# The first two token groups of a fused attention and expert kernel take turns in halves, with an order table found beforehand

## Chip, cores and metric

The kernel runs on one core of a Trainium2 chip. The metric is the device time of one execution in microseconds (us); the median of several runs is quoted. Engines are named as the profile names them: PE is TensorE (matmuls), PEld its weight loads, DVE is VectorE, ACT is ScalarE, POOL is GpSimd, SP is SyncE, which issues nearly all DMAs.

## What is computed

Attention with a compressive memory on 4 batches, 8 heads, 576 tokens and head size 64, followed by a gated expert layer on the 2304 tokens:

```
a       = softmax(causal(q k^T / 8));   local = a v
q_p     = phi(q)                        # phi(x) = elu(x) + 1
mem_out = (q_p M_prev) / (q_p z_prev)
x       = sigmoid(beta) * mem_out + (1 - sigmoid(beta)) * local     # [2304, 512]
out     = (sigmoid(x Wg) * (x Wv)) Wo                               # d_ff = 1536, out [2304, 512]
```

The expert weights arrive as 64-bit floats and are converted on the chip.

## The kernel before

**Work.** The 2304 tokens are cut into 6 groups of 384. Groups 1 to 4 are the first 384 tokens of each batch; groups 0 and 5 are "tail" groups that join the last 192 tokens of two batches. Attention of a group goes by 4 pairs of heads, 24 pairs (numbers 0 to 23) in all. For each pair `scores` (L577 matmuls in plain f32) writes scores to PSUM banks, DVE masks and takes the row extreme (L641), ACT takes the exponential (L653), the result is turned, `values` multiplies by v (L336), `scaled` normalises into `xs` with the small row factors `rs`, `recall` does the same for the memory term `xm` (row factors `rn`). `across` turns the finished 384x128 block into `xh` and `xl`, a high and a low half in the fast 32-bit matmul format, for the expert layer. For pairs 0 to 7 both turns go through PE (L339, against the identity `idn`), for pairs 8 to 23 through DMA transposes (`planes`).

**Experts.** A group then takes 12 expert steps of 128 hidden units each (`moe`). A step is 33 matmuls: 12 for the gate and 12 for the value (128x384, high and low halves of `x` and of the weights), and 9 for the output product ("down", 128x512), which accumulate over all 12 steps in three PSUM banks (0 to 2), one for each 128 tokens. Between them ACT takes a tanh and DVE and ACT make `th`, `gh`, `gl` (L941, L943, L345, L355). The down matmuls of a step stand after the gate and value matmuls of the next one. At a group's end the three sums go through ACT to `ob`, a ring of two buffers, and out by DMA. Group 0 and the last group go through the three sums in the order 2, 0, 1, the others 0, 1, 2.

**Weights.** In group 0 each step's three weight blocks are loaded and converted (`convert`: one ACT pass, L850, L852 and L855 on DVE, then a split into halves by a cast on ACT and a subtraction on DVE). The gate weights `wg` stay in SBUF; value and output weights live in a ring `sv` of three buffers, and their converted f32 form is written to DRAM (`w`). Later groups load it back (`sv<-w`, 512 KB) and split it again. Groups go through the steps upwards and downwards by turns, so that the three last steps' buffers are still there for the next group.

**Order.** The code records every operation in `Program` with an engine, a cost, the data it depends on and a place in the order. A list scheduler then goes through it: whenever an engine is free, the ready operation with the lowest place goes next, and the engines' instruction queues are emitted in that order. In the kernel before, a search at build time (`plan`, `replay`, `issue`) moves places to and fro against three modelled worlds (`SEARCH`, `WORLDS`) and keeps the best. The recording loop at the end of the program interleaves attention of group g+1 with the expert steps of group g, paced so that it is done when the 12 steps are.

Of the kernel before, what the change touches and what calls it, by code (L numbers as in the profile page):

```python
# [25 lines left out]
AHEAD = 8  # L26


# [6 lines left out]
ROUNDS = 1  # L35

SEARCH = (260.0, 1500), (1e9, 300)

WORLDS = (380.0, 1.2, 0.0, 0.0), (385.0, 1.2, 0.03, 0.6), (370.0, 1.2, 0.03, 1.2)
# [14 lines left out]
class Program:  # L54
# [63 lines left out]
    def plan(self, order, until):  # L118

        ops, cost, kbs, engine, users = self.ops, self.cost, self.kbs, self.engine, self.users  # L120
        rate, lag, _, _ = self.worlds[0]
        push, pop = heapq.heappush, heapq.heappop
        left = list(self.left)
        ready_at = [0.0] * len(ops)
        free = [START] * 5
        link = 0.0
        coming, ready = [[] for _ in range(5)], [[] for _ in range(5)]
        for i, n in enumerate(left):
            if not n:
                push(coming[engine[i]], (0.0, i))  # L130
        made = []
        while True:
            at, e = 1e9, -1
            for x in range(5):
                t = free[x]
                if not ready[x]:
                    c = coming[x]
                    if not c:
                        continue
                    if c[0][0] > t:  # L140
                        t = c[0][0]
                if t < at:
                    at, e = t, x
            if e < 0 or free[PE] > until:
                return made
            c, r = coming[e], ready[e]
            while c and c[0][0] <= at:
                k = pop(c)[1]
                push(r, (order[k], k))
            i = pop(r)[1]  # L150
            done = at + (cost[i] * 1.5 if e == PE and at < COLD else cost[i])
            free[e] = done
            if kbs[i]:
                link = done = max(link, done + lag) + kbs[i] / rate
            made.append(i)
            for u, wake in users[i]:
                t = done + wake
                if t > ready_at[u]:
                    ready_at[u] = t
                left[u] -= 1  # L160
                if not left[u]:
                    push(coming[engine[u]], (ready_at[u], u))

    def replay(self, made, world):

        rate, lag, costs, lates = world
        kbs, engine, users, pe = self.kbs, self.engine, self.users, self.cost
        n = len(self.ops)
        ready_at, start, last = [0.0] * n, [0.0] * n, [-1] * n
        free = [START] * 5  # L170
        link = 0.0
        cold = COLD
        rest = self.work
        gaps = []
        for i in made:
            e = engine[i]
            at = ready_at[i]
            c = costs[i]
            if e == PE:
                rest -= c  # L180
                if at < free[PE]:
                    at = free[PE]
                else:
                    gap = at - free[PE]
                    if gap > 0.1:
                        gaps.append((gap, i))
                        if gap > 1.3:
                            cold = max(cold, at + 2.0)
                if at < cold:
                    c *= 1.5  # L190
            elif at < free[e]:
                at = free[e]
            start[i] = at
            free[e] = done = at + c
            if kbs[i]:
                link = max(link, done + lag) + kbs[i] / rate
                done = link + lates[i]
            for u, wake in users[i]:
                t = done + wake
                if t > ready_at[u]:  # L200
                    ready_at[u], last[u] = t, i
        return max(max(free), free[PE] + rest), gaps, start, ready_at, last

    def issue(self):
        ops = self.ops
        names = sorted(WAKE)
        self.cost, self.kbs = [o[1] for o in ops], [o[2] for o in ops]
        self.engine, self.left = [names.index(o[0]) for o in ops], [len(o[4]) for o in ops]
        self.users = [[] for _ in ops]
        for i, o in enumerate(ops):  # L210
            for d in o[4]:
                self.users[d].append((i, WAKE[ops[d][0]][o[0]]))
        self.work = sum(o[1] for o in ops if o[0] == "pe")
        pick = random.Random(1)
        self.worlds = [(rate, lag, [o[1] * (1.0 + pick.random() * slip if o[0] in ("act", "dve", "pool") else 1.0) for o in ops],
                        [pick.random() ** 2 * late for _ in ops]) for rate, lag, slip, late in WORLDS]

        def trial(order, until, bar):
            made = self.plan(order, until)
            runs = []  # L220
            for w in self.worlds:
                runs.append(self.replay(made, w))
                if sum(r[0] for r in runs) > sum(bar[:len(runs)]) + (len(runs) < len(self.worlds)):
                    return None
            return [r[0] for r in runs], made, runs

        order = [o[5] for o in ops]
        for until, rounds in SEARCH:
            best = trial(order, until, [1e9] * len(self.worlds))
            for _ in range(int(rounds * ROUNDS)):  # L230
                _, gaps, start, ready_at, last = pick.choice(best[2])
                if not gaps:
                    continue
                _, i = pick.choices(gaps, [x for x, _ in gaps])[0]
                late = []
                end = start[i] - 25.0
                while i >= 0 and start[i] > end:
                    if start[i] - ready_at[i] > 0.05:
                        late.append(i)
                    i = last[i]  # L240
                if not late:
                    continue
                tried = list(order)
                for k in pick.sample(late, pick.randint(1, min(3, len(late)))):
                    by = pick.choice((20, 60, 150, 400))
                    for m in self.mates[k]:
                        tried[m] -= by
                now = trial(tried, until, best[0])
                if now:
                    best, order = now, tried  # L250
        for i in best[1]:
            ops[i][3]()
        self._best = best
        return sum(best[0]) / len(best[0])
# [3 lines left out]
def tile_attention_memory_moe(  # L258
# [522 lines left out]
    def attn():  # L781
# [10 lines left out]
        for n, x in [(n, x) for n in range(NP) for x in range(len(pairs[n].items))] + [(NP, 0)]:  # L792
# [17 lines left out]
            while len(late) > (SKEW if n < HP else n < NP):  # L810
# [3 lines left out]
                if x == len(pairs[k].items) - 1:  # L814
# [12 lines left out]
                    for y in ks:  # L827
                        across(y)
# [35 lines left out]
    def weights(F):  # L864

        g, at = divmod(F, NF)
        if g >= NG:
            return
# [199 lines left out]
```

## Time and profile before

| | us |
|---|---|
| median of 3 runs | 617.55 |
| lowest and highest run | 617.44, 620.86 |
| the profiled execution | 618.01 |
| its span, first to last instruction | 616.2 |
| PE busy in it | 603.3 (98%) |
| DVE busy | 457.9 (74%) |
| ACT busy | 316.6 (51%) |

The profiled execution ran 0.46 us longer than the median, and 1.8 us of it lie around the span. Busy time of PE counts a matmul from its start to its modelled end, and matmuls overlap: a 128x384 matmul shows 0.34 us, while the next one starts 0.17 us later. So the pace of PE is read from the starts.

### The profile page before, as it was taken

How to read it: one execution, taken by the hardware profiler on the slowest of the kernel's cores; microseconds unless marked ns; L12 is line 12 of the kernel's file. 1: busy time of each engine (PE TensorE's matmuls, PEld its weight loads, DVE VectorE, ACT ScalarE, POOL GpSimd, SP SyncE). 2: the span in 40 equal slices, each digit the busy share in tenths (PEclk: the TensorE clock that was granted, in tenths of full speed). 3: DMA queues.
4: the chain of work that ended last, by engine and by line, in shares of the span. 5: the costliest groups of instructions: out<-in, count | busy, mean ns of one | idle time of the engine just before them, and what ended most of it. 6: DMA issues, size and time to landing. Idle time of an engine off the chain costs nothing.

```text
span 616.2 us, 13289 instructions
## 1 busy us (share of the span) xinstructions
PE 603.3 (98%) x5184; PEld 528.7 (86%) x5184; DVE 457.9 (74%) x1181; ACT 316.6 (51%) x626; POOL 9.0 (1%) x51
## 2 busy tenths in 40 slices
PE   6899999999999999999999999999999999999997
PEld 3668889888888988898988899978898889999996
DVE  4899999999988777577789568689889965223432
ACT  6897867757545255245366236274555333322322
POOL 2000000000000000000000000000000000000000
PEclk9999999999999999999999999999999999999999
DMA  8578778897869454455474575668596652112231
GB/s 323 195 235 295 212 226 234 254 249 224 176 130 243 104 152 122 120 150 145 106 162 111 126 168 137 138 155 161 127 206 105 154 133 69 54 48 101 69 102 53
DMA packets 110623, 96.60 MB, mean 157 GB/s; under 512 B 79840, under 2 KB 81888, under 8 KB 110560
## 3 DMA queue, kind: packets, MB, share of 16 engines
q1 hardware_dynamic: 110416, 95.48, 59.8%
q8 instruction: 41, 0.67, 0.4%
q10 hardware_dynamic: 144, 0.26, 0.1%
q14 instruction: 22, 0.18, 0.1%
HBM read 65.84 MB, written 11.01 MB: 125 GB/s over the span
## 4 chain that ended last, share of the span: by engine, by line
PE 90%; DVE 5%; ACT 2%; issue 0%; DMA 0%; DVEq 0%
PE bank L332 75%; PE bank L336 7%; PE bank L577 5%; PE bank L339 2%; DVE a L641 1%; PE bank L534 1%; ACT a L653 1%; DVE sv L355 1%; DMA w<-wt 0%; DVE wt L852 0%; DVE xm L355 0%; DVE wt L855 0%; DVE xs L355 0%; ACT at L345 0%; DVE kq_wt L355 0%
## 5 line engine op out<-in xcount | busy, mean ns | idle before, releaser
L332 PE MATMUL bank<-xh,sv 128*128 128x384 f32 x576 | 163.3, 339 | 0.0
L332 PE MATMUL bank<-xh,wg 128*128 128x384 f32 x576 | 162.7, 340 | 0.1
L332 PE MATMUL bank<-sv,gh 128*128 128x512 f32 x432 | 138.2, 399 | 0.0
L332 PEld LDWEIGHTS bank<-xh,wg 128*128 128x128 f32 x576 | 105.3, 188 | 5.2 <-issue 0.5
L332 PEld LDWEIGHTS bank<-xh,sv 128*128 128x128 f32 x576 | 105.3, 188 | 2.1 <-issue 0.5
L943 DVE SCALAR_TENSOR_TENSOR th<-th,bank 128x384 f32<-128x384 f32 x72 | 39.8, 553 | 84.3 <-PE bank L332 84.1
L653 ACT ACTIVATE a<-a,st 128x256 f32<-128x256 f32 (+4 forms) x144 | 78.2, 580 | 39.2 <-DVE st L641 38.5
L332 PE MATMUL bank<-xl,wg 128*128 128x384 f32 x288 | 97.3, 338 | 0.0
L332 PE MATMUL bank<-xl,sv 128*128 128x384 f32 x288 | 97.0, 337 | 0.0
L666 DVE COPY at<-a 128x1024 uint16<-128x1024 uint16 (+1 forms) x144 | 86.1, 628 | 7.8 <-DMA a<-at 5.7
L332 PEld LDWEIGHTS bank<-sv,gh 128*128 128x128 f32 x432 | 79.0, 188 | 15.1 <-issue 1.0
L345 ACT CAST gh<-th 128x384 fp32r<-128x384 f32 x72 | 36.8, 512 | 97.2 <-DVE th L943 97.0
L332 PE MATMUL bank<-sv,gl 128*128 128x512 f32 x216 | 86.5, 401 | 0.0
L641 DVE CUSTOM_DVE_ANT_0 a<-bank,mask 128x512 f32<-128x512 f32 (+3 forms) x144 | 65.9, 489 | 13.1 <-PE bank L577 10.3
L941 ACT ACTIVATE th<-bank 128x384 f32<-128x384 f32 x72 | 35.2, 489 | 77.8 <-PE bank L332 75.8
L345 ACT CAST sv<-sv 128x512 fp32r<-128x512 f32 x90 | 51.2, 616 | 16.8 <-DMA sv<-w 16.5
L577 PE MATMUL bank<-kp 64*64 64x256 f32 (+4 forms) x416 | 53.8, 443 | 5.1 <-DMA kp<-in_qk_dram 4.1
L355 DVE TENSOR_TENSOR sv<-sv 128x512 fp32r<-128x512 f32 x90 | 58.1, 687 | 0.6 <-ACT sv L345 0.3
L332 PEld LDWEIGHTS bank<-xl,wg 128*128 128x128 f32 x288 | 54.1, 188 | 2.8
L355 DVE TENSOR_TENSOR gl<-th,gh 128x384 fp32r<-128x384 f32 x72 | 40.1, 557 | 19.9 <-ACT gh L345 19.1
L332 PEld LDWEIGHTS bank<-xl,sv 128*128 128x128 f32 x288 | 54.1, 188 | 0.3
L332 PEld LDWEIGHTS bank<-sv,gl 128*128 128x128 f32 x216 | 40.5, 188 | 9.3 <-DVE gl L355 0.2
(66 smaller groups left out, 600.8 us busy)
## 6 DMA issues: line engine op xcount, KB each, us to landing
sv<-w SPq DMA_DIRECT2D x45, 512.0 KB, 3.9
wr<-in_w_dram SPq DMA_DIRECT2D x36, 512.0 KB, 4.8
kp<-in_qk_dram SPq DMA_DIRECT2D x32, 384.0 KB, 3.8
w<-wt SPq DMA_DIRECT2D x24, 256.0 KB, 5.1
out_dram<-ob SPq DMA_DIRECT2D x14, 256.0 KB, 2.3
vt<-in_vp_dram SPq DMA_DIRECT2D x8, 330.0 KB, 3.7
vr<-in_vp_dram SPq DMA_DIRECT2D x8, 330.0 KB, 4.4
mb<-in_mz_dram SPq DMA_DIRECT2D x8, 260.0 KB, 5.0
```

Of the source, the lines that this page charges most:

```text
L332: lambda: nc.tensor.matmul(out=out, lhsT=lhsT, rhs=rhs, start=start, stop=stop), r, w)
L336: lambda: nc.tensor.matmul(out=out, lhsT=lhsT, rhs=rhs, start=start, stop=stop), r, w)
L339: pe(0.110, lambda: nc.tensor.transpose(out=out, in_=in_, identity=identity), r, w)
L345: act(n, lambda: nc.scalar.copy(out=out, in_=in_), r, w)
L355: dve(n, lambda: nc.vector.tensor_tensor(out=out, in0=in0, in1=in1, op=op), r, w)
L534: nc.tensor.matmul(out=sp[j][0][m0:m1, at + MC * c:at + MC * c + MC], lhsT=u.ph[r, q:q + m1 - m0], rhs=mem[u.g][e][0][r, u.p, MC * j:MC * ...
L577: nc.tensor.matmul(out=sp[j][0][m0:m1, at:at + k1 - k0], lhsT=kp[r, u.qa + q:u.qa + q + m1 - m0], rhs=kp[r, u.ka + k0:u.ka + k1], start=Tr ...
L641: dve(m + 10, lambda aj=aj, sj=sj, pj=pj, o=o, m=m, mk=mk, b=b0 + k0: nc.vector.tensor_tensor_reduce(out=aj[:, b:b + m], in0=pj[:, o:o + m ...
L653: act(W + 120, lambda aj=aj, sj=sj, b=b0, W=W: nc.scalar.activation(out=aj[:, b:b + W], in_=aj[:, b:b + W], func=AF.Exp, scale=-1.0, bias= ...
L666: dve(2 * W, lambda: nc.vector.tensor_copy(out=o, in_=i), r, w, fast=True)
L941: act(GT, lambda: nc.scalar.activation(out=th, in_=pg_[:, :GT], func=AF.Tanh, scale=0.5), [pg_k], [th_k])
L943: dve(GT, lambda: nc.vector.scalar_tensor_tensor(out=th, in0=th, scalar=1.0, in1=pv[:, :GT], op0=ALU.add, op1=ALU.mult,), [th_k, pv_k], [t ...
```

## The change

Groups 0 and 1 no longer do 12 steps each in one go. The expert work becomes a list of stages: group 0 steps 0 to 5; group 1 steps 5 to 0; group 0 steps 6 to 11; group 1 steps 11 to 6; then groups 2 to 5 with 12 steps each. A stage that only opens a group writes its three half-way sums to a DRAM buffer (`halves`); the stage that closes it loads them into `ob` and adds them to its own sums on DVE. Conversion of a weight block happens at its first use, so it is spread over four stages. `sv` buffers are now given out by least recent use. Attention of group 1 has to be complete after 6 steps of group 0; `across` of group 2 (`held`) waits until group 0 has closed, since there are two `xh` and `xl` buffers. Two modelled PE costs change, the search is gone, and a table of numbers (`MOVED`) shifts the places of single operations.

```diff
-SEARCH = (260.0, 1500), (1e9, 300)
-WORLDS = (380.0, 1.2, 0.0, 0.0), (385.0, 1.2, 0.03, 0.6), (370.0, 1.2, 0.03, 1.2)
+CUT = 6
+LINK = 380.0, 1.2
+MOVED = {
+        -6400: (1275,),
+        -800: (1202, 1276, 1700, 4596),
...
-                    pe(4 * at / 2385.0 + (0.8 if more else 0.3), together,
+                    pe(4 * at / 2385.0 + (0.36 if more else 0.32), together,
...
+        def over():
+            while held and freed:
+                across(held.pop(0))
+                yield
...
+                yield from over()
+                while held and n == 2 * HP + HP - 1:
+                    yield "wait"
+                    yield from over()
                 scores(n, x)
...
-                    for y in ks:
-                        across(y)
+                    if pairs[k].g == 2:
+                        held.extend(ks)
+                        yield from over()
+                    else:
+                        for y in ks:
+                            across(y)
...
+    low, high = list(range(CUT)), list(range(CUT, NF))
+    stages = [(0, low, True, False), (1, low[::-1], True, False), (0, high, False, True), (1, high[::-1], False, True)]
+    stages += [(g, (high + low, low[::-1] + high[::-1])[g % 2], True, True) for g in range(2, NG)]
...
+        if f in kept:
+            at = kept.index(f)
+            turns_w.remove(at)
+            turns_w.append(at)
+            ready_w[F] = next(ready_w[x] for x in range(F - 1, -1, -1) if steps_[x][1] == f)
             return
...
-        if g == 0:
+        if f not in seen:
+            seen.add(f)
...
+    halves = [dram.tile([128, GT // 128, DM], F32, name=f"part{g}") for g in range(2)]
+
+    def moe(n):
+        g, fs, opens, closes = stages[n]
...
+            if not opens:
+                load(o, halves[g][:, t], 256, [("part", g, t)], [ob_k])
+                dve(DM, lambda o=o, acc=acc: nc.vector.scalar_tensor_tensor(
+                    out=o, in0=acc, scalar=0.5, in1=o, op0=ALU.mult, op1=ALU.add), [acc_k, ob_k], [ob_k])
+                for r, q, m in rows(g, t):
+                    load(out[r:r + m, :], o[q:q + m], 2.1 * m, [ob_k], [])
+                continue
...
+            if not closes:
+                load(halves[g][:, t], o, 256, [ob_k], [("part", g, t)])
+                continue
```

The number of PE instructions is the same in both programs, kind by kind. Of the others, six casts on ACT and six subtractions on DVE for `sv`, and three loads `sv<-w`, are gone; six additions on DVE, six stores to and six loads from the half-way buffers are new.

Three places show how instructions move. The first is the start of PE's queue, after the first eight score matmuls of pair 0 (`kp0`, `kp1`). `a0` to `a5` are the exponentials, `bank` the PSUM banks, and `kp2` belongs to pair 1. Before:

```order
L339 MATMUL bank0_63<-idn_71,a0_112 128x128 x4
L339 MATMUL bank1_64<-idn_71,a1_113 128x128 x4
L577 MATMUL bank2_65<-kp2_103 128x512
L577 MATMUL bank3_66<-kp2_103 128x512
L339 MATMUL bank4_67<-idn_71,a2_116 128x128 x3
L577 MATMUL bank6_69<-kp0_101 64x256
L577 MATMUL bank7_70<-kp0_101 64x256
L577 MATMUL bank6_69<-kp1_102 64x256
L577 MATMUL bank7_70<-kp1_102 64x256
```

And now:

```order
L285 MATMUL bank0_63<-idn_71,a0_114 128x128 x4
L285 MATMUL bank1_64<-idn_71,a1_115 128x128 x3
L523 MATMUL bank6_69<-kp0_103 64x256
L523 MATMUL bank7_70<-kp0_103 64x256
L523 MATMUL bank6_69<-kp1_104 64x256
L523 MATMUL bank7_70<-kp1_104 64x256
```

The last scores of pair 0 (64x256, banks 6 and 7) now stand ahead of the first scores of pair 1. On SP the load of `bt` (beta, for the gates `gs` and `ga`) has moved as well, from the ninth place to the sixth.

The second place is DVE's queue where the last two pairs of group 1 (pairs 6 and 7) are normalised, from the first row factor `rs` on. Before:

```order
L516 SCALAR_TENSOR_TENSOR rs1_145<-bank6_69,ga_76 128x6
L516 SCALAR_TENSOR_TENSOR rs0_131<-bank5_68,ga_76 128x6
L666 COPY at0_127<-a4_120 128x512
L850 TENSOR_SCALAR wt3_148<-wt3_148 128x512
L355 TENSOR_TENSOR sv2_152<-wt2_143,sv2_152 128x512
L852 SCALAR_TENSOR_TENSOR wt3_148<-wr0_138,wt3_148 128x512
L520 RECIPROCAL rs0_131<-rs0_131 128x6
L520 RECIPROCAL rs1_145<-rs1_145 128x6
L855 SCALAR_TENSOR_TENSOR wt3_148<-wr0_138,wt3_148 128x512
L850 TENSOR_SCALAR wt0_139<-wt0_139 128x512
L355 TENSOR_TENSOR xs0_130<-bank5_68,rs0_131 128x384
L852 SCALAR_TENSOR_TENSOR wt0_139<-wr1_140,wt0_139 128x512
```

And now:

```order
L462 SCALAR_TENSOR_TENSOR rs0_133<-bank5_68,ga_76 128x6
L814 SCALAR_TENSOR_TENSOR wt3_150<-wr1_142,wt3_150 128x512
L466 RECIPROCAL rs0_133<-rs0_133 128x6
L301 TENSOR_TENSOR sv2_154<-wt1_143,sv2_154 128x512
L301 TENSOR_TENSOR xs0_132<-bank5_68,rs0_133 128x384
L462 SCALAR_TENSOR_TENSOR rs1_147<-bank6_69,ga_76 128x6
L612 COPY at0_129<-a4_122 128x512
L301 TENSOR_TENSOR xs0_132<-xs0_132,xm0_126 128x384
L466 RECIPROCAL rs1_147<-rs1_147 128x6
L612 COPY at0_129<-a5_123 128x512
L301 TENSOR_TENSOR xs1_146<-bank6_69,rs1_147 128x384
L922 SCALAR_TENSOR_TENSOR th0_151<-th0_151,bank4_67 128x384
```

Fewer pieces of weight conversion (`wt`, `sv`) stand between the parts of the normalisation. From the first `rs` to the second `xl` of these pairs the queue holds 27 instructions before, and 21 now, the one-column reads not counted.

The third place is SP's queue where group 0 is closed. Before:

```order
L671 DMA_TRANSPOSE a4_120<-at3_136 128x8x128
L363 DMA out_0_dram<-ob0_157 64x512 x2
L363 DMA out_0_dram<-ob1_158 128x512
L671 DMA_TRANSPOSE a5_121<-at3_136 128x8x128
L363 DMA out_0_dram<-ob0_157 128x512
L363 DMA vt0_108<-in_vp_dram 128x396
L363 DMA sv2_152<-w8_85 128x2x512
```

And now:

```order
L309 DMA out_0_dram<-ob0_159 64x512 x2
L309 DMA out_0_dram<-ob1_160 128x512
L309 DMA ob0_159<-part0_101 128x512
L309 DMA ob1_160<-part1_102 128x512
L309 DMA out_0_dram<-ob0_159 128x512
L309 DMA kp3_106<-in_qk_dram 128x768
L309 DMA sv0_139<-w8_85 128x2x512
```

The third half-way sum of group 0 (`part0`) is loaded into the first `ob` buffer once that one's store has landed; its own store then stands ahead of the load of k and q for a later pair and of the next weights.

## Rows read from the trace of the kernel before

**Rows 1.** The page: span, and PE's busy time, share of the span, instructions.

```profile
span 616.2 us, 13289 instructions
PE 603.3 (98%) x5184; PEld 528.7 (86%) x5184; DVE 457.9 (74%) x1181; ACT 316.6 (51%) x626; POOL 9.0 (1%) x51
```

**Rows 2.** One stretch of 20 us: busy us of PE, PEld, DVE, ACT, POOL; granted clock, DMA share, GB/s.

```profile
80.00:100.00 20.00, 20.00 (x222) 17.66 (x222) 20.00 (x55) 14.07 (x29) 0.22 (x2) 1.00 0.80 237
```

**Rows 3.** Waits of PE over the span: us in total, times, longest.

```profile
PE bank L577 <- DMA kp<-in_qk_dram: 4.1, 1, 4.1
PE bank L339 <- ACT a L653: 1.6, 3, 1.1
PE bank L332 <- DVE xm L355: 0.9, 1, 0.9
PE bank L339 <- DVE xs L355: 0.6, 1, 0.6
PE bank L577 <- DVE xm L355: 0.6, 1, 0.6
PE bank L577 <- DVE st L641: 0.3, 1, 0.3
PE bank L577 <- DVE xl L355: 0.2, 1, 0.2
```

**Rows 4.** Timeline of PE, the last matmul: start, us, instruction.

```profile
611.30 0.40 PE L332 MATMUL bank<-sv,gl 128*128 128x512 f32 x1
```

**Rows 5.** Timeline of PE, one step of the last group: its first matmul, the next step's.

```profile
546.64 0.33 PE L332 MATMUL bank<-xh,wg 128*128 128x384 f32 x1
...
552.95 0.33 PE L332 MATMUL bank<-xh,wg 128*128 128x384 f32 x1
```

**Rows 6.** Timeline from 14 to 18 us; in brackets the wait before.

```profile
14.80 0.44 PE L339 MATMUL bank<-idn,a 128*128 128x128 f32 x2 [1.14 <-ACT a L653]
...
15.47 1.09 PE L339 MATMUL bank<-idn,a 128*128 128x128 f32 x8 [0.23 <-ACT a L653]
15.79 0.21 ACT L395 ACTIVATE gs<-bt 128x8 f32<-128x8 f32 x1
...
17.14 1.39 PE L577 MATMUL bank<-kp 64*128 64x512 f32 x4 [0.57 <-DVE xm L355]
```

**Rows 7.** Groups of instructions: count, then busy us and mean ns.

```profile
L345 ACT CAST sv<-sv 128x512 fp32r<-128x512 f32 x90 | 51.2, 616 | 16.8 <-DMA sv<-w 16.5
...
L355 DVE TENSOR_TENSOR sv<-sv 128x512 fp32r<-128x512 f32 x90 | 58.1, 687 | 0.6 <-ACT sv L345 0.3
```

**Rows 8.** Timeline of the hand-over of pairs 6 and 7 to the experts.

```profile
124.56 1.57 PE L336 MATMUL bank<-vr,at 128*64 128x66 f32 x48
126.73 0.23 DVE L516 SCALAR_TENSOR_TENSOR rs<-bank,ga 128x6 f32<-128x6 f32 x2
...
137.96 0.55 DVE L355 TENSOR_TENSOR xl<-bank,xh 128x384 fp32r<-128x384 f32 x1
```

**Rows 9.** Timeline where group 0 closes: the sums leave, the next group's begin.

```profile
162.22 1.14 ACT L960 ACTIVATE ob<-bank 128x512 f32<-128x512 f32 x2
...
162.56 0.62 PE L332 MATMUL bank<-sv,gh 128*128 128x512 f32 x2
164.10 1.83 SPq L363 DMA_DIRECT2D out_dram<-ob  x3
...
167.63 0.59 ACT L960 ACTIVATE ob<-bank 128x512 f32<-128x512 f32 x1
...
169.68 0.62 PE L332 MATMUL bank<-sv,gh 128*128 128x512 f32 x2
```

**Rows 10.** DMA issues: count, KB each, median us from issue to landing.

```profile
sv<-w SPq DMA_DIRECT2D x45, 512.0 KB, 3.9
...
w<-wt SPq DMA_DIRECT2D x24, 256.0 KB, 5.1
```

**Rows 11.** The stretch around the one late wait of PE, columns as in rows 2.

```profile
405.00:420.00 15.00, 14.12 (x102) 11.61 (x102) 14.80 (x41) 9.80 (x20) 0.00 (x0) 1.00 0.56 159
```

More of the change, by code (lines that the diff above doesn't have):

```diff
@@ L116, in block @@
         self.turn = None
[L118 to L202, printed above, removed]
@@ L206, in issue @@
         names = sorted(WAKE)
-        self.cost, self.kbs = [o[1] for o in ops], [o[2] for o in ops]
-        self.engine, self.left = [names.index(o[0]) for o in ops], [len(o[4]) for o in ops]
-        self.users = [[] for _ in ops]
+        rate, lag = LINK
+        push, pop = heapq.heappush, heapq.heappop
+        order = [o[5] for o in ops]
+        for by, firsts in MOVED.items():
+            for i in firsts:
+                for m in self.mates[i]:
+                    order[m] += by
+        left = [len(o[4]) for o in ops]
@@ L210, in issue @@
+        users = [[] for _ in ops]
         for i, o in enumerate(ops):
             for d in o[4]:
[L212 to L254, printed above, removed]
+                users[d].append(i)
+        ready_at = [0.0] * len(ops)
+        free = [START] * len(names)
+        link = 0.0
+        coming, ready = [[] for _ in names], [[] for _ in names]
+        for i, n in enumerate(left):
+            if not n:
+                push(coming[names.index(ops[i][0])], (0.0, i))
+        while any(coming) or any(ready):
+            at, e = min((free[x] if ready[x] else max(free[x], coming[x][0][0]), x)
+                        for x in range(len(names)) if ready[x] or coming[x])
+            while coming[e] and coming[e][0][0] <= at:
+                k = pop(coming[e])[1]
+                push(ready[e], (order[k], k))
+            i = pop(ready[e])[1]
+            _, cost, kb, emit, _, _ = ops[i]
+            done = at + (cost * 1.5 if e == PE and at < COLD else cost)
+            free[e] = done
+            if kb:
+                link = done = max(link, done + lag) + kb / rate
+            emit()
+            for u in users[i]:
+                x = names.index(ops[u][0])
+                ready_at[u] = max(ready_at[u], done + WAKE[names[e]][names[x]])
+                left[u] -= 1
+                if not left[u]:
+                    push(coming[x], (ready_at[u], u))
@@ L779, in across @@
         keys.append([kh, kl])
+    freed = []
     def attn():
@@ L916, in down @@
                     matmul(acc, l[:, ts], r, DM, [l_k, r_k], [acc_k],
[L917 removed]
+                           f == fs[0] and i == 0, f == fs[-1] and i == 2)
                 yield
[L920 to L922 removed]
+        for at, f in enumerate(fs):
+            cur = ready_w[firsts[n] + at]
+            pz = [bank("second" if n == 0 and at == 1 else "gv") for _ in range(2)]
             turns = [(part, kd) for part in range(2) for kd in range(KD)]
[L924 removed]
+            if opens and at == 0 or n == 0 and at == 1:
                 turns = [x for x in turns if x[1] < KD - 1] + [x for x in turns if x[1] == KD - 1]
[L927 removed]
+            for m, (part, kd) in enumerate(turns):
                 pp, pp_k = pz[part]
@@ L993, in tile_attention_memory_moe @@
     lengths = [sum(2 * len(u.items) + 4 for u in pairs if u.g == g) for g in range(1, NG)] + [0]
-    def pace(g, part):
-        return sum(lengths[:g]) + part * lengths[g]
-    for g in range(NG):
+    for n, (g, fs, _, closes) in enumerate(stages):
         while ready < g:
@@ L1003, in tile_attention_memory_moe @@
                 ready = y[1]
-        for i, _ in enumerate(moe(g)):
-            while made < pace(g, (i + 1) / (7 * NF + 1)) + AHEAD and ready + 1 < NG:
+        if n < 4:
+            done_, todo = (0, lengths[0]) if n == 0 else (lengths[0], lengths[1])
+            f0, f1 = (0, CUT) if n == 0 else (firsts[n] - CUT, NF + NF - CUT)
+        else:
+            done_, todo = sum(lengths[:g]), lengths[g]
+            f0, f1 = 0, NF
+        if n == 3:
+            freed.append(True)
+        for i, _ in enumerate(moe(n)):
+            share = (f0 + (i + 1) / 7) / f1
+            while made < done_ + share * todo + AHEAD and ready + 1 < NG:
                 made += 1
                 y = step()
+                if y == "wait":
+                    break
                 if y:
```

32 lines of the change are left out of this document (14 added, 18 removed), and 39 rows, old and new, of the table MOVED.

## Prediction

> **What bounds the kernel now.** I read the page's busy line first. PE is busy for 603.3 of the 616.2 us of the span [rows 1], so the kernel can't get much faster unless PE gets less to do. The stretches of 20 us come next. From 60 to 600 us nearly all of them look like the one shown: PE 20.00 of 20 [rows 2]. DVE is just as full there, 20.00 of 20, but that costs nothing while PE has other work at hand. The third view is the list of PE's waits. The reader is to add it up: 4.1 us until the first keys and queries land, and after that 1.6 + 0.6 + 0.6 + 0.3 + 0.2 = 3.3 us in the first 50 us and 0.9 us at 415 us [rows 3]. The last matmul ends at 611.70 [rows 4], 4.5 us before the span does. So 4.1 + 3.3 + 0.9 + 4.5 = 12.8 us, which is the whole of 616.2 - 603.3. The start and the tail are in both programs. What any order can win is 4.2 us, 0.7%.
>
> Is busy time also time well spent? In the last group, with no attention left, a step takes 552.95 - 546.64 = 6.31 us [rows 5]. 72 steps at that pace are 454 us, and the order shows the same matmuls before and after. I take PE's work as unchanged.
>
> **The change part by part.** *Weights.* Three loads `sv<-w` less, and with each two casts and two subtractions: ACT loses 6 x 0.616 = 3.7 us, DVE 6 x 0.687 = 4.1 us [rows 7], and DVE gets six additions of 512 columns, 6 x 0.69 = 4.1 us, back. Conversion is spread over 24 steps in place of 12. Through the stretch in which DVE is full, PE doesn't wait at all [rows 2, 3], so a relief of DVE there is worth 0 by itself. It is cover for what the change moves forward (below).
>
> *The start.* Three of the early waits come from one knot [rows 6]. PE waits 1.14 and 0.23 us for exponentials of pair 0 whose last scores were issued behind the first scores of pair 1. Then it waits 0.57 us for banks 6 and 7, because `xm` reads them late: its gate `gs` starts on ACT only at 15.79. In the new order those scores stand ahead of pair 1's, and `bt` is loaded earlier. Both causes are gone: 1.94 us. What is late next is the first transpose of pair 1, with much the same chain behind it; I keep the other early waits (3.3 - 1.94 = 1.4) and the late 0.9, 2.3 together, as they are, less 0.5, because DVE and ACT now have less conversion ahead of the first expert step. Bounds: none of it gone (0) or all (2.3).
>
> *Group 1 is due six steps earlier.* That is 6 x 6.31 = 38 us. The last two pairs' values end on PE at 126.13, and their second `xl` on DVE ends at 138.51 [rows 8]: 12.4 us, hidden, since group 1's experts began much later. Now the order leaves between the same two points 27 gate and value matmuls, 4 down matmuls, 6 transposes and 4 score matmuls. A step's 6.31 us are about 0.175 us for each of its 24 gate and value matmuls and 0.23 for each of its 9 down matmuls; 8 transposes take 1.09 us [rows 6]. That makes 4.7 + 0.9 + 0.8, and with about 1 us for the scores 7.5 us. DVE's part shrinks from 27 instructions to 21: in proportion to the 138.51 - 126.73 = 11.8 us that the 27 took, 21 take 9.2 us, and fewer of them are conversion pieces at 0.69, so I estimate 8. The first `rs` may start 1.5 us before the values end, since it needs only the first pair's bank (half of two blocks of about 1.57). 8 - 1.5 + 0.5 of hand-over is 7.0, against 7.5. I take 0.3 us of wait. Bounds: 0, and 12.4 - 7.5 = 4.9 if DVE arrives with the backlog of before. What is queued behind on DVE are `th` and `gl` of the steps, for which PE waits next, so a late DVE isn't caught up by reordering: the order is fixed.
>
> *Half-way sums.* At a closing the third sum needs a buffer whose store has landed, then a load, then DVE. Before, at the same place, the third sum is out of its bank at 168.22, and PE wants a bank of that kind again at 169.68 [rows 9]. The last sums' matmuls begin at 162.56; about 0.7 later they end, so the store's way took 168.22 - 163.2 = 5.0 us. The load adds between 3.9 us (512 KB) and 5.1 us (256 KB) [rows 10], the addition 0.1 more than the evacuation. So the bank is free 9.0 to 10.2 us after the last down matmul, plus 0.3 of hand-over. The new order puts 41 gate and value matmuls, three down matmuls and a block of scores between, 7.2 + 0.7 + about 0.9 = 8.8 us. The wait is 0.5 to 1.7 us. It shrinks by up to 1.3 us if SP isn't busy with transposes when the first sum is ready; before, that held the store from 162.8 to 164.10 [rows 9]. In the new queue no transpose stands just ahead. I take 0.5, bounds 0 and 1.7. At group 1's closing the order leaves over 12 us, and I take 0. The two openings only store: 0, hidden as the evacuation of rows 9 is.
>
> Here a rule speaks. The Trainium skill ("DMA: Bandwidth & Descriptors", "Anatomy of one DMA — SWDGE (gpsimd) path") gives a DMA about 2.0 us and its bytes at 436 GB/s; it states it for GpSimd's path, these go through SP. By it a 256 KB load is 2.6 us, an estimate from that page, and the wait would be 0; the trace's 5.1 us for as many bytes, with other traffic in flight, differs.
>
> *Sum*, against the profiled execution: 618.01 - 1.94 - 0.5 + 0.3 + 0.5 = 616.4, and from the median, 0.46 us lower, 617.55 - 1.64 = 615.9 us. A difference under 1% (6.2 us) is about what a measurement of this kernel can't tell from no change.
>
> **The rivals.** *All waits go.* 617.55 - 4.2 = 613.3. For it: DVE and ACT are less loaded early, and the table moves hundreds of places, so it was made for this order. Against: the early attention is a chain of scores, extreme, exponential, turn, with only two pairs in flight, and it waits on each link in turn.
>
> *Nothing is gained.* The chain of the early attention is as long as before, and the 1.94 us come back at its next link: 617.55 + 0.3 + 0.5 = 618.4; with the borders hidden, 617.5. For it: the later waits of rows 3 name other links of that chain (DVE `xs`, DVE `st`).
>
> *DVE is late at the border of the first two stages: slower.* If it comes to `rs` with the backlog of before, PE stands 4.9 us there, and 1.7 at the closing: 617.55 - 1.94 + 4.9 + 1.7 = 622.2. It decides from about 1.9 us of lateness on, where the gain of the start is used up. For it: DVE was at 20.00 of 20 [rows 2] and the border is now inside that stretch. Against: six of the twelve conversions are no longer due by then.
>
> On the clock, the trace shows the granted clock at 1.00 (the 2.4 GHz level) also in the stretch with the wait of 0.9 us [rows 11], so waits of about a microsecond cost only themselves. By the Trainium skill ("TensorE: Matmul & The Clock Gate", "HAM oscillation — how this bites in real kernels") a long enough gap sends PE back to half its clock. No wait here after the start is longer than 1.14 us, so no run shows it. By that rule the slower case would cost some us more, as PE would go on at 1.2 GHz after the gap.
>
> **How the numbers follow.** Forecast, 614.4 to 617.0: 0.45. Nothing gained, 617.0 to 619: 0.20. All waits gone, under 614.4: 0.17. Slower, 619 and up: 0.18. Faster by over 1% means under 611.4, which would need more than all of PE's avoidable waits: 0.04, from the third case and PE's work being read wrongly. Slower by over 1% is above 623.7, the slower case with a second such wait: 0.08. Within 1%: 0.88. The range 612.6 to 621.0 leaves out the far ends of the third and the fourth case, together some 0.17.
>
> **What would show it.** Right: PE's busy time within 2 us of 603.3, its waits between 10 and 20 us down by about 2 us, the step of the last group still 6.31 us, waits of at most 1 us at the first border and at group 0's closing, granted clock 1.00. The steps are wrong one by one if the early waits still sum to 3.3; if PE waits for `xs`, `xl` or `th` for 2 us or more near 115 us; if it waits for `ob` near 180 us. The whole is wrong if PE's busy time changes by more than 4 us, since the argument rests on equal work.

## Result, and the profile after

The changed kernel takes 610.32 us (median of 5 runs, 610.13 to 611.24), the one before 617.93 us beside it (617.44 to 620.86): ratio 0.988, 95% interval 0.986 to 0.990. That is 1.2% faster, where faster by over 1% had a chance of 0.04, and 2.3 us under the lower end of the predicted range. The profiled execution took 611.24 us, the longest of the five, so the two profiles lie 6.8 us apart and the medians 7.6.

The page's first lines of after, which answer to [rows 1]:

```profile
span 609.5 us, 13288 instructions
PE 598.1 (98%) x5184; PEld 528.4 (87%) x5184; DVE 459.0 (75%) x1181; ACT 309.9 (51%) x620; POOL 8.4 (1%) x51
```

The span is 6.8 us shorter (616.23 and 609.45 before rounding), and 5.2 us of that are PE's *busy* time, 603.3 before [rows 1], with the same 5184 matmuls and weight loads that take as long as before (528.4 against 528.7). So PE counts as busy for longer in before, on the same work. The waits of PE in after, as in [rows 3]:

```profile
PE bank L523 <- DMA kp<-in_qk_dram: 4.1, 1, 4.1
PE bank L285 <- DVE xs L301: 0.9, 1, 0.9
PE bank L523 <- ACT at L291: 0.9, 1, 0.9
PE bank L285 <- DVE st L587: 0.9, 1, 0.9
```

Behind the first load 2.7 us are left of 4.2. This view explains 1.5 of the 6.8 us.

What the view leaves out is seen in the starts. Two stops of the kernel before, in its timeline of PE (start, us, instruction; a row with x2 holds two matmuls):

```profile
148.91 0.63 PE L332 MATMUL bank<-sv,gh 128*128 128x512 f32 x2
149.37 0.40 PE L332 MATMUL bank<-sv,gl 128*128 128x512 f32 x1
149.73 0.98 PE L332 MATMUL bank<-sv,gh 128*128 128x512 f32 x3
...
539.72 0.33 PE L332 MATMUL bank<-xl,sv 128*128 128x384 f32 x1
539.90 0.34 PE L332 MATMUL bank<-xh,sv 128*128 128x384 f32 x1
540.29 0.44 PE L332 MATMUL bank<-xh,wg 128*128 128x384 f32 x1
540.57 0.34 PE L332 MATMUL bank<-xl,wg 128*128 128x384 f32 x1
540.75 0.51 PE L332 MATMUL bank<-xh,wg 128*128 128x384 f32 x2
```

Matmuls of 384 columns start 0.17 us apart. After 539.90 the next one starts 0.39 later, and the one after that 0.28 later: 0.33 us are lost, of which the trace counts 0.06 as idle. At 149.37 it is 0.36 in place of 0.23, and no wait is listed. A matmul's end is modelled; when PE runs dry, the modelled end covers a part of the stop. At four stops among expert matmuls the trace counts some idle time (0.01, 0.88, 0.01 and 0.06 us at 52.95, 413.95, 421.99 and 539.90 us; only the 0.88 stands in the list of waits). Each lost 0.27 us more than that.

So I took the span apart by starts alone: each interval to the next start, less 0.231 us for 512 columns or 0.174 for 384 where the matmul is an expert's (the 32 score matmuls in the fast format are counted with those).

| us | before | after | |
|---|---|---|---|
| first expert matmul starts | 52.00 | 48.25 | -3.75 |
| from there to the last matmul's start | 559.30 | 556.30 | -3.00 |
| of this: late starts among expert matmuls | 4.07 | 1.84 | -2.23 |
| expert matmuls beside an attention block (78, 70 blocks) | 12.55 | 11.87 | -0.68 |
| the attention matmuls' own intervals (2162) | 85.17 | 85.07 | -0.10 |
| from the last start to the end of the span | 4.93 | 4.90 | -0.03 |

Both ends of the first row in the timelines, of before:

```profile
52.00 0.42 PE L332 MATMUL bank<-xh,wg 128*128 128x384 f32 x1
```

and of after, with its last matmul and one step of the last group (552.56 - 546.25 = 6.31, as in [rows 5]):

```profile
48.25 0.42 PE L278 MATMUL bank<-xh,wg 128*128 128x384 f32 x1
...
546.25 0.33 PE L278 MATMUL bank<-xh,wg 128*128 128x384 f32 x1
...
552.56 0.33 PE L278 MATMUL bank<-xh,wg 128*128 128x384 f32 x1
...
604.55 0.39 PE L278 MATMUL bank<-sv,gl 128*128 128x512 f32 x1
```

In these two profiles somewhat more than half of the gain falls ahead of the first expert matmul, the rest behind it. Behind it DVE and ACT are less busy than before. From 60 to 160 us, columns as in [rows 2], before:

```profile
60.00:160.00 100.00, 100.00 (x851) 87.70 (x849) 99.09 (x264) 69.78 (x139) 1.97 (x8) 1.00 0.80 229
```

and after:

```profile
60.00:160.00 100.00, 100.00 (x956) 87.88 (x955) 95.68 (x272) 66.17 (x135) 0.66 (x6) 1.00 0.81 220
```

DVE was 0.9 us short of full and is 4.3 us short now; ACT loses 3.6 us.

### The profile page after: what moved, and what is told of

Read it like the earlier page. It is cut to its first block, busy times and chain, and to the rows that moved or that the text cites. A ratio compares the mean times of both kernels' runs of the same rounds, so it can differ in the third digit from the quotient of the medians.

```text
span 609.5 us, 13288 instructions
## 1 busy us (share of the span) xinstructions
PE 598.1 (98%) x5184; PEld 528.4 (87%) x5184; DVE 459.0 (75%) x1181; ACT 309.9 (51%) x620; POOL 8.4 (1%) x51
## 4 chain that ended last, share of the span: by engine, by line
PE 94%; ACT 2%; DVE 1%; DMA 1%; SPq 1%; issue 0%; POOL 0%
PE bank L278 77%; PE bank L282 8%; PE bank L523 6%; PE bank L285 3%; PE bank L480 1%; DMA vt<-in_vp_dram 1%; ACT a L599 1%; SPq L309 1%; ACT at L291 1%; DVE a L587 0%; DVE wt L814 0%; DVE wt L817 0%; DVE xs L301 0%; DVE wt L812 0%; DVE sv L301 0%
## 5 line engine op out<-in xcount | busy, mean ns | idle before, releaser
L278 PE MATMUL bank<-xh,wg 128*128 128x384 f32 x576 | 165.2, 341 | 0.0
L599 ACT ACTIVATE a<-a,st 128x512 f32<-128x512 f32 (+3 forms) x144 | 77.8, 582 | 26.5 <-DVE st L587 26.1
L278 PE MATMUL bank<-sv,gl 128*128 128x512 f32 x216 | 84.7, 395 | 0.0
L587 DVE CUSTOM_DVE_ANT_0 a<-bank,mask 128x512 f32<-128x512 f32 (+3 forms) x144 | 64.6, 483 | 20.4 <-PE bank L523 12.8
L523 PE MATMUL bank<-kp 64*64 64x256 f32 (+4 forms) x416 | 51.5, 442 | 5.0 <-DMA kp<-in_qk_dram 4.1
L301 DVE TENSOR_TENSOR sv<-sv 128x512 fp32r<-128x512 f32 x84 | 54.3, 686 | 0.0
L291 ACT CAST sv<-sv 128x512 fp32r<-128x512 f32 x84 | 47.7, 616 | 5.2 <-DMA sv<-w 5.2
```

Source lines behind the costliest of these rows:

```text
L278: lambda: nc.tensor.matmul(out=out, lhsT=lhsT, rhs=rhs, start=start, stop=stop), r, w)
L291: act(n, lambda: nc.scalar.copy(out=out, in_=in_), r, w)
L301: dve(n, lambda: nc.vector.tensor_tensor(out=out, in0=in0, in1=in1, op=op), r, w)
L523: nc.tensor.matmul(out=sp[j][0][m0:m1, at:at + k1 - k0], lhsT=kp[r, u.qa + q:u.qa + q + m1 - m0], rhs=kp[r, u.ka + k0:u.ka + k1], start=Tr ...
L587: dve(m + 10, lambda aj=aj, sj=sj, pj=pj, o=o, m=m, mk=mk, b=b0 + k0: nc.vector.tensor_tensor_reduce(out=aj[:, b:b + m], in0=pj[:, o:o + m ...
L599: act(W + 120, lambda aj=aj, sj=sj, b=b0, W=W: nc.scalar.activation(out=aj[:, b:b + W], in_=aj[:, b:b + W], func=AF.Exp, scale=-1.0, bias= ...
```

## Experiments

Theories: **A**, the gain is in the order, which has fewer stops; **B**, the turns give it, by taking conversion out of the first stretch; **C**, the new costs of the attention matmuls do. Medians below are in us; before took 617.3 to 617.8 beside them. Diffs that stand for a search or an order are outlines: from the long search on, such a kernel issues an order that was found beforehand and is written out in it as a list.

**No found order.** After with an empty table, before with no search.

```diff
-MOVED = {
...
+MOVED = {}
```
```diff
-ROUNDS = 1
+ROUNDS = 0
```

> The stages of after with an empty table: the scheduler's own order, no search. Theory A (the gain is in the order: fewer places where PE stops, each costing more than the idle time it shows): most of the 7 us go, 615 to 622 us, with more and longer PE waits than the 2.7 us (after the start) of after. Theory B (the turns themselves give the time, by taking half of the conversion out of the first stage and by fewer reloads): within 2 us of after, 609 to 612 us.

> Before with no search rounds: the scheduler's own order on the old program. With the run above it prices the turns without any order found by search. Theory A: 622 to 632 us, and within 3 us of the run with turns and plain order. Theory B: at least 5 us slower than the run with turns and plain order.

Measured: 624.05 with turns (ratio to before 1.009, 1.007 to 1.012), longer than both theories had it, and 622.41 without (1.007, 1.005 to 1.008), as theory A had it. Theory B in its plain form is out: turns by themselves are no gain. The waits of the run with turns name the reason:

```profile
PE bank L236 <- ACT xh L249: 4.7, 1, 4.7
```

One stop, which ends at 543.8 us where the last group begins. Its stretches (columns as in [rows 2]; the granted clock stands behind POOL):

```profile
540.00:545.00 5.00, 1.16 (x3) 0.85 (x4) 1.16 (x2) 0.51 (x1) 0.00 (x0) 0.67 0.21 39
545.00:550.00 5.00, 5.00 (x21) 4.87 (x20) 1.11 (x2) 1.46 (x3) 0.00 (x0) 0.65 0.00 0
550.00:555.00 5.00, 5.00 (x28) 4.60 (x27) 1.11 (x2) 0.55 (x2) 0.00 (x0) 1.00 0.03 6
```

Within the 4.7 us the granted clock falls to its lower level (1.2 GHz, half speed); it stays there until some 548 us, and matmuls start 0.32 us apart in place of 0.17. By starts this one stop cost 7.2 us. Elsewhere the turns were ahead: first expert matmul at 51.70 against 54.34 us, and 566.4 - 7.2 = 559.2 us behind it against 561.6. That is 5 us, but not all of it is the turns': in the profile without them the clock fell too, behind two stops of 1.18 and 0.74 us:

```profile
45.00:50.00 5.00, 3.78 (x44) 3.24 (x46) 5.00 (x16) 4.72 (x10) 0.00 (x0) 0.73 0.54 197
```

That kernel's three executions with a granted clock of 0.999 or more took 620.16 to 620.80 us, against 624.05 - 7.2 = 616.85. So turns gave some 3.3 to 4 us and one bad hand-over took them back.

**The old search on the turns; the new costs in before.**

```diff
-MOVED, LINK and issue of after
+ROUNDS, SEARCH, WORLDS, plan, replay and issue of before
```
```diff
-                    pe(4 * at / 2385.0 + (0.8 if more else 0.3), together,
+                    pe(4 * at / 2385.0 + (0.36 if more else 0.32), together,
```

> The stages and costs of after with the search of before in place of the table. Theory B: 609 to 612.5 us, since the turns give the time with any decent order. Theory A in its strict form (only the table's order has it): 614 to 619 us. Between them, both have a share. In each case PE's excess over after should be found as waits and as stops among matmuls, not as slower matmuls.

> Before with its own search, only the two constants of the attention matmul's cost changed, 0.8 and 0.3 to 0.36 and 0.32, as in after. Theory C (the better costs let the same search find the better order): at least 3 us faster, 611 to 615 us. Theories A and B: within 2 us of before, 616 to 620 us.

Measured: 614.79 (ratio 0.995, 0.993 to 0.997) with turns, in the range of A's strict form, and 622.69 (1.008, 1.006 to 1.011) without, longer than any theory had it. Theory C is out: the new costs alone are worse. With them, the same search is 7.9 us better on the turns; with its own costs before is 2.8 us behind.

**The same long search on both.** The same moves, 27 times as many, from the programs' own places; the order found is written out as a list and issued.

```diff
-        for i in best[1]:
+        for i in MADE:
             ops[i][3]()
```

> The old program, no turns, with its own costs; the same search taken 27 times as far (40000 and 10000 trials in place of 1500 and 300), its order written out. Theory A1 (any good order does it, with or without turns): 609 to 612.5 us, level with after. Theory AB (the turns leave room that an order can use and the old program hasn't got; the gain needs both): 614 to 617 us, well short of after.

> The stages of after with the same long search, the costs of after. Theory A1: level with the old program under the long search, within 1.5 us. Theory AB: at least 3 us faster than that one, 608 to 612 us, PE waits after the start about 2 to 3 us and the first expert matmul before 50 us.

Measured: 617.35 (0.999, 0.998 to 1.001) and 613.63 (0.992, 0.990 to 0.994). A longer search buys the old program nothing, against A1, and the turns are 3.7 us better under it, at least 3 as AB had it; both times lie above AB's ranges, by 0.4 and 1.6 us. The first expert matmuls start at 50.65 and 49.49 us, and DVE from 60 to 160 us is busy for 99.27 and 95.33 us.

**A search that is told of stops.** The search's replay adds 0.2 us for each stop and 0.1 us for each change between attention and expert matmuls; the new costs on both programs.

```diff
+            if gap > 0: at += 0.2
+            if kind != last_kind: at += 0.1
```

> The old program with the costs of after (which by themselves gave 622.7 us) and a long search whose price for a stop of PE is its idle time and 0.2 us, and 0.1 us for a change between attention and expert matmuls. If hidden costs of stops and changes are real and of that size, it is faster than the old program under the long search without them, by 0.5 to 2 us (fewer attention blocks among the experts, 69 against 75). If they are not: level within 0.5 us or slower. Theory AB says it doesn't get under 612.5 us, theory A1 that it does.

> The stages of after with the same long search and the same prices for stops and changes. Theories AB and of hidden stop costs: 607 to 611 us, at or under after, and at least 3 us under the old program with these prices. Theory A1: within 1.5 us of it.

Measured: 618.86 (1.002, 1.000 to 1.004) and 616.42 (0.996, 0.994 to 0.997). Neither expectation on the price held: both are slower than the long search without it (for the old program the costs differ as well). What stays is that the turns win by 2.4 us where costs and search are the same. That difference understates the turns: five of their nine executions had a granted clock of 0.996 and took 616.4 to 616.8 us, the other four 614.35 to 614.70. Between executions at 0.999 or more the medians are 618.63 and 614.38, 4.25 us apart.

**Starts exchanged.** Everything up to the first expert matmul is issued in the other kernel's order.

```diff
-        for i in MADE_OWN:
+        for i in START_OF_OTHER + [x for x in MADE_OWN if x not in START_OF_OTHER]:
             ops[i][3]()
```

> The stages of after; everything that before issues ahead of its first expert matmul is issued in before's order, the rest in the order of after. Theory S: first expert matmul at 51.5 to 52.5 us, time 613 to 615 us, from the first expert matmul to the last one 556 to 557 us as in after. Rival R: that stretch changes by 1 us or more.

> The old program (no turns); everything that after issues ahead of its first expert matmul is issued in after's order, the rest in the order of before. Theory S (3.75 us of the gain are the order of the first 50 us alone and need no turns): first expert matmul at 48 to 49 us in place of 52.0, time 613 to 615 us, the stops later on as in before. Rival R (the early order is bought with work put off, conversions above all, which the old program has no room for): the first expert matmul comes early, but new stops after it give at least half back, 615.5 to 619 us.

After with the start of before: 615.46 (0.996, 0.994 to 0.997). Its first expert and last matmul:

```profile
52.18 0.45 PE L385 MATMUL bank<-xh,wg 128*128 128x384 f32 x1 [0.46 <-ACT at L398]
...
608.77 0.39 PE L385 MATMUL bank<-sv,gl 128*128 128x512 f32 x1
```

The start moves by 3.9 us, and 608.77 - 52.18 = 556.59 us behind it are after's 556.30: the two parts of the gain are separate, as theory S says; the time lies 0.5 us above its range. By medians the old start costs 615.46 - 610.32 = 5.1 us, two thirds of the whole gain (before took 617.53 and 617.93 beside them). The profiles show less, since after's began late (48.25 us, against 46.94 to 47.67 in three other profiles with its start); 0.46 us is a wait at the seam. The other way round it didn't come out: 620.40 (1.004, 1.002 to 1.006), in no theory's range.

```profile
46.31 1.47 PE L388 MATMUL bank<-idn,a 128*128 128x128 f32 x12
52.64 0.69 PE L381 MATMUL bank<-xh,wg 128*128 128x384 f32 x1 [4.86 <-ACT at L394]
```

PE is through the early attention by 47.8 us, about as in after (48.3), and then stands 4.86 us, since ACT has conversions of the old order ahead of the copy `at` that ends the wait. Behind the stop the granted clock is at its lower level:

```profile
53.00:54.00 1.00, 1.00 (x4) 1.00 (x4) 1.00 (x3) 1.00 (x3) 0.00 (x0) 0.50 0.52 147
```

That is the seam between two orders as much as the old program, so the order was searched again from this start:

> The old program again, no turns, old costs: the search starts from after's order for everything ahead of the first expert matmul (before's for the rest), and goes on for 100000 and 30000 trials with 0.2 us per stop, so that the rest is fitted to the new start. Theory S with AB (the start's gain needs no turns, the later one does): first expert matmul at 48.5 to 50.5 us, stops at 140 to 160 us remain, time 613 to 615.5 us. Theory A1 (with a good enough order the old program is level with after): 609.5 to 612 us. Theory R (the old program can't have that start without paying for it later): 616 to 619 us.

> The kernel of before_searched_from_new_start once more, for a profile of an undisturbed execution. Theory R (the new start is paid for later): first expert matmul at 48.5 to 50.5 us, and from there to the last matmul 561 us or more in place of 559.3. Else, if the start itself didn't come out: first expert matmul after 51 us.

Measured: 619.47 (1.002, 1.001 to 1.004), above all three ranges, and 619.80 (1.003, 1.002 to 1.005) the second time. In the second profile the first expert matmul starts at 52.97 us, so the start itself didn't come out. The search had moved the start again, for a new stop of 0.86 us at 7 us among others. Whether the old program can have after's start stays open; three searched orders of it began at 50.65, 52.97 and 54.36 us, the last (the search told of stops) in an execution of 622.57 us whose granted clock was 0.50 from 17 to 23 us.

**The price of a change.** In after, plain-f32 matmuls of zeros in the middle of each step's down matmuls, in the same bank.

```diff
+            for _ in range(more):      # 1, then 4, once in each of 72 steps
+                nc.tensor.matmul(out=out[0:64, 0:65], lhsT=idn[0:64, 64:128], rhs=idn[0:64, 0:65], start=False, stop=False)
```

> After, with one plain-f32 matmul of zeros (64x65) in the middle of each expert step's down matmuls, added to the same bank: 72 more. Theory H (each change from expert matmuls to plain f32 and back has a price of its own, 0.2 to 0.35 us, as read from the starts): 14 to 25 us more, 625 to 636 us. Rival (it costs its own pace only, 0.01 to 0.06 us, and what the trace shows at the changes is how ends are modelled): 0.5 to 4 us more, 611 to 614.5 us.

> The same with four such matmuls in a row at the same 72 places. Theory H: the change is paid once, so at most 72 x 3 x 0.03 = 6.5 us above the run with one. If the price goes by the matmul and not by the change: four times the excess of that run.

Measured: 642.40 (1.039, 1.036 to 1.042) and 667.34 (1.079, 1.075 to 1.083). One costs (642.40 - 610.32) / 72 = 0.45 us, each further one (667.34 - 642.40) / 216 = 0.115 us. So by subtraction 0.33 us are the change there and back, within theory H's 0.2 to 0.35; but a further one costs more than the 0.03 allowed, and both times lie above H's ranges. In the timeline of the run with one (a plain-f32 matmul shows as two records):

```profile
584.39 0.63 PE L278 MATMUL bank<-sv,gh 128*128 128x512 f32 x2
584.95 0.33 PE L280 MATMUL bank<-idn 64*64 64x65 f32 x2
585.20 0.50 PE L278 MATMUL bank<-sv,gl 128*128 128x512 f32 x1
585.54 0.63 PE L278 MATMUL bank<-sv,gh 128*128 128x512 f32 x2
```

The `gl` and the `gh` behind it would start at 584.85 and 585.08; the latter starts at 585.54, 0.46 late, and the waits list none of it. For this change it explains little: after has 8 blocks less among its expert matmuls, yet by starts only 0.68 + 0.10 us came of that. A likely reason, not tested, is that a block which joins another one still changes between kinds of attention matmuls.

**A lighter DVE, same order.** Every engine's instructions stay where they are; the last DVE step of a conversion does a quarter of its columns.

```diff
-            out=t, in0=lo, scalar=29, in1=t, op0=ALU.logical_shift_right, op1=ALU.bitwise_or,
+            out=t[:, :128], in0=lo[:, :128], scalar=29, in1=t[:, :128], op0=ALU.logical_shift_right, op1=ALU.bitwise_or,
```

> Before, instruction for instruction in its own order; only the last step of each weight conversion on DVE (the low bits, 36 instructions of 0.687 us in the first 200 us) does 128 of the 512 columns, so the low bits of the other columns are left out. DVE loses some 36 x 0.4 = 14 us there. Theory D (the stops of the old program up to 160 us come from a full DVE, which is what the turns relieve): at least 2 us faster, 612 to 615.5 us, the stop at 149 us gone and the first expert matmul at least 1 us earlier. Rival (the stops are the attention chain's own length and order, DVE's fullness costs PE nothing, as the prediction had it): within 1 us of before, 616.5 to 618.5 us.

> After with the same conversion work left out, its order unchanged. Theory D: after has already what a lighter DVE gives, so it gains less than half of what before gains: 0 to 1.5 us, 609 to 610.5 us. Rival: also within 1 us, and as much as before.

Measured: before 615.52 (0.996, 0.995 to 0.998), after 610.87 (0.989, 0.987 to 0.990 against before). The group of DVE in the lighter before, and its stretch and first expert matmul:

```profile
L904 DVE SCALAR_TENSOR_TENSOR wt<-wr,wt 128x128 int32<-128x128 int32 x36 | 10.2, 283 | 0.1
```
```profile
60.00:160.00 100.00, 100.00 (x876) 88.59 (x876) 91.69 (x265) 71.53 (x144) 1.97 (x8) 1.00 0.80 227
```
```profile
50.46 0.42 PE L381 MATMUL bank<-xh,wg 128*128 128x384 f32 x1
```

36 x (0.687 - 0.283) = 14.5 us less on DVE give the old kernel 615.52 - 617.78 = -2.3 us: 1.54 before the first expert matmul, 0.92 behind it, where the late starts at 53 and 149 us are gone. After gains nothing by it. Both times lie just above theory D's ranges (by 0.02 and 0.4 us), but the old kernel's gain of over 2 us, its earlier start, the stop gone at 149 us and the missing gain in after are D's signs and not the rival's: a full DVE cost before some 2 us, and after doesn't pay that. The run doesn't separate a DVE with more room from weights that are each ready 0.4 us sooner, and the split into 1.54 and 0.92 rests on one profile each.

**On from after's order.** The long search from the table's own order, 0.2 us for a stop and 0.05 us for a change.

```diff
-        order = [o[5] for o in ops]
+        order = places of after, with MOVED applied
```

> The stages of after; the search goes on from after's own order, with 0.2 us per stop and 0.05 us per change between attention and expert matmuls. If orders near after's still hold something that such a price sees: 608 to 610 us, first expert matmul up to 0.5 us earlier. If after's order is as good as this search can tell: 610 to 612 us, level with after.

Measured: 612.16 (0.990, 0.988 to 0.992), just above both ranges, with the first expert matmul at 48.60 us. Nothing beat after; an order close to it is 1.8 us slower.

## Why the prediction was wrong, step by step

**The step that failed** stands in its first part: "What any order can win is 4.2 us, 0.7%", with "I take PE's work as unchanged" behind it. The work was unchanged, the busy time wasn't. Waits listed behind the first load fell by 1.5 us (4.2 to 2.7), where the sum had 1.94 + 0.5; the other 5.2 us came out of 603.3 us that I had called spent. Each of the four stops above loses 0.27 us beyond the idle time counted, some stops have none counted, and in the start most of what was won lay in intervals without idle time. I had read that matmuls' ends are modelled and used it for the pace of a step, but not for the waits. The prediction had named this as what would make it wrong, PE's busy time changing "by more than 4 us": it changed by 5.2.

The Trainium skill says this ("Perfetto Trace Analysis", "Tensor Engine Instruction (MATMUL, LD_WEIGHTS)"): the profiler computes a matmul's end from its size, so it is a model and no measurement; and "Identifying the Most-Contended Engine" there calls matmul busy time a poor measure of how near a kernel is to its limit and points to the weight loads. The trace agrees: busy time fell by 5.2 us, the weight loads' by 0.3.

**Weights**: "a relief of DVE there is worth 0 by itself" was wrong. With the order unchanged, 14.5 us less on DVE gave before 2.3 us, and after none. Three loads less and six additions more balance, as said: DVE's total is 459.0 against 457.9 us.

**The start**, 1.94 + 0.5 us by the sum, was 3.75. The three waits of [rows 6] are gone as forecast, but three of 0.9 us stand at other links, so the listed waits up to the first expert matmul only fell from 3.38 to 2.75 us. By starts, 1.0 us of the 3.75 lies where PE went idle, 9 times before and 5 times now. The other 2.7 us lie in intervals with no idle time: PE changes there 32 times before, and 24 times now, between matmuls of scores, transposes, values and memory. That this is the reason is argued; no run changes it alone. A wait at a transpose costs more than it lists there too (1.42 us from 13.39 to 14.80 for a listed 1.14, where 0.11 is its pace). The bounds "none of it gone (0) or all (2.3)" were bounds of the listed time, and so too narrow.

**Group 1 due earlier**: right. The hand-over, in the timeline of after:

```profile
106.27 1.57 PE L282 MATMUL bank<-vr,at 128*64 128x66 f32 x48
108.31 0.15 DVE L462 SCALAR_TENSOR_TENSOR rs<-bank,ga 128x6 f32<-128x6 f32 x1
...
114.45 0.55 DVE L301 TENSOR_TENSOR xl<-bank,xh 128x384 fp32r<-128x384 f32 x1
```

From the values' end at 107.84 to `xl`'s at 115.00 it is 7.2 us, where the forecast was 7.0 and the kernel before took 12.4; PE doesn't wait (0.3 forecast).

**Half-way sums**: 0.5 us of wait forecast, none measured. DVE waited 1.0 us once for a half-way sum, PE for nothing. The new transfers (issues, KB each, median us to landing):

```profile
part<-ob SPq DMA_DIRECT2D x6, 256.0 KB, 3.3
ob<-part SPq DMA_DIRECT2D x6, 256.0 KB, 4.0
```

4.0 us for a load of 256 KB lies at the lower end of the 3.9 to 5.1 that I took. The 2.6 us that I estimated from the Trainium skill's rule ("DMA: Bandwidth & Descriptors", "Anatomy of one DMA — SWDGE (gpsimd) path") also led to no wait, but the measured load is 1.4 us longer.

**The rivals.** "All waits go", 613.3, was nearest and still 3.0 us too high, for the same reason. "Nothing is gained" had the chain's next links right and their price wrong. The slower one didn't come. That waits of about a microsecond "cost only themselves" holds at 415 us [rows 11], but not everywhere: behind stops of 1.18 and 0.74 us (no found order, without turns) and of 0.79, 0.45 and 0.66 us (the search told of stops, without turns) the granted clock fell to its lower level. In the profiles of before and after it didn't. Right in detail were the last group's step of 6.31 us, the tail, and a granted clock of 1.00 from 60 to 160 us.

**What the gain is made of.** By medians 5.1 us hang on the order ahead of the first expert matmul; whether that order needs the turns is open. With the same costs and the same search the turns are worth 7.9 us under the old search, and 2.4 us under the one with stop prices (4.25 at equal granted clock); 3.7 us under the long search, where each program had its own costs. 3.3 us more lie between that order on the turns and the table's. How the table was found isn't known. That DVE's relief is how the turns help is shown for about 2 of the us by the lighter conversion; for the rest of their share it is argued.

## What to carry to other kernels

Where the bound engine's ends are modelled, add up its starts: interval by interval against the engine's own best pace, and see which stop costs how much, before saying what an order can win. An engine that is full for a hundred microseconds beside the bound one isn't free, even with no wait listed against it. And judge a restructuring together with an order searched for it: here the turns came out 1.6 us slower without a found order, of which one stop was 7.2 us, and 2.4 to 7.9 us faster under equal searches.

## What the runs showed of the hardware

A stop of PE among expert matmuls loses about 0.27 us beyond its idle time (four stops in before): the next matmul starts late and the one behind it is 0.11 us late again, and this counts as busy. One change from expert matmuls to plain f32 and back costs 0.33 us by subtraction, though no wait is listed. A stop of 4.7 us late in a run took 7.2 us, since the granted clock fell to its lower level in it; the stop of 0.9 us at 415 us in before left it at 1.00 [rows 11]. With stops of 0.79, 0.45 and 0.66 us close together it fell, in the start of the old program searched with stop prices:

```profile
17.00:20.00 3.00, 2.85 (x10) 1.02 (x12) 0.25 (x2) 1.07 (x3) 0.00 (x0) 0.50 0.20 76
```

And the same start order began its expert matmuls at 46.94, 47.66, 47.67 and 48.25 us in four profiles, so a start read from one profile is uncertain by up to 1.3 us.
